# The first of two rank mixes, issued in two halves among the second batch's attention heads

## The chip, the core and the metric

The program runs on one core of a Trainium2 chip. The core has a matrix engine (TensorE, PE in the profile, with its weight loads as PEld), a vector engine (DVE), a scalar engine (ACT), a general engine (POOL) and an engine that here only issues transfers (SP). The four compute engines each take their own list of instructions in order and wait for one another by semaphores. PE writes only to PSUM, a small memory of eight banks, from which DVE and ACT fetch results. The metric is the device time of one execution in microseconds; the kernel before took 1562.12 us as the median of three runs (1556.07 to 1563.89).

## What is computed

Four batches of 448 tokens and 12 heads of width 64 go through attention with normalised queries and keys, then through two mixers. The first mixer adds a low-rank mix over the tokens (rank 32) and then a two-layer network over the 768 channels; the second has a 256-wide token network and a second channel network.

```python
q_n, k_n = rmsnorm(q, g_q), rmsnorm(k, g_k)
attn = softmax(q_n @ k_n.T / 8)            # 4 batches x 12 heads, 448 x 448
x = attn @ v                               # as (4, 448, 768)
u = x + ((x.T @ U) @ V).T                  # the rank mix, U 448x32, V 32x448
x = u + relu(u @ w_ch1) @ w_ch2            # 768 -> 3072 -> 768
u = x + (relu(x.T @ w_tok1) @ w_tok2).T
x = u + relu(u @ w_ch1b) @ w_ch2b          # 768 -> 1536 -> 768
```

The weights arrive as 64-bit floats, and the kernel turns each piece into a pair of 32-bit numbers, a high and a low part.

## The kernel before, in words

Batches are called first to fourth here, heads are counted from 0 over all batches, so heads 0 to 11 are the first batch's and heads 12 to 23 the second's. `attention` walks the heads one step at a time. In step t it issues the softmax of head t+1 (`softmax`: four tiles of scores `sc`, a maximum `nm` on DVE L334, the exponential `p` on ACT L336, and on POOL the scaling L343) next to the weighing of head t (`weigh`: transposes of `p` into `pt`, copies `ph` and `pl` by ACT and DVE, products `pv`), and every second step it loads and normalises a pair of heads ahead of time. The result goes into `xT`, channels by tokens, six pieces of 128 channels; the pieces 0 to 2 are heads 0 to 5 of a batch, the pieces 3 to 5 are heads 6 to 11.

`rank_mix` works in two halves of three pieces. Per half: four times three transposes of `xT` into PSUM (`pt_x`, L432), each evicted as a high part by ACT (L438) and a low part by DVE (L439); two products each into `ps_h`; a copy of `ps_h` by ACT (L461) and a subtraction by DVE (L462); six products into three tiles `ps_u`; and for each of these an addition into `xT` on DVE (L443), a copy `u` on ACT (L444) and a subtraction on POOL (L445).

In the part of the program that matters here, the heads 0 to 23 run first, alone, with PSUM pools `s` (three banks, for `sc`), `t` (one) and `p` (four, for `pt` and `pv`). The factors U and V (`uv`) are loaded in step 8 and sit in two of the four pairs of weight buffers `wh`/`wl`. After step 23 these pools are closed, others are opened with two banks in `p` and two in `s`, and both rank mixes are issued, the first batch's and then the second's. Then `ffn` begins with the first group of the channel network: two pieces of its first weight (`w1_chunk`), two of its second (`w2_chunk`), products `ps_g` for the first batch and then `ps_x`, while the third batch's heads go on among them. A weight piece is made by `to_f32` and `split`: ACT L125 and L130, DVE L126, L127 and L131, POOL L134, then ACT L144 and POOL L145. Since `uv` holds two of the four weight buffers, the two `w2` pieces go into the buffers that the U factors and the V factors leave, which is after the last `ps_h` and after the last `ps_u` of the second rank mix.

The order of the instructions on each engine is not the order of the code. A scheduler decides it at build time by its own estimate of when each instruction can run. Buffers, PSUM banks among them, are handed out in the order of the code, so a tile that is asked for later waits until the earlier holders of its buffer are done.

Of the kernel before, what the change touches and what calls it, by code (L numbers as in the profile page):

```python
# [10 lines left out]
F32R = mybir.dt.float32r  # L11
# [13 lines left out]
def attention_then_two_mixers(  # L25
# [31 lines left out]
    P = 128  # L57
    B, H, S, D = q.shape
# [7 lines left out]
    HALF = DM // 2  # L66
# [8 lines left out]
    def f(x):  # L75
        return x.bitcast(F32)

    def mm(o, l, r, start, stop):
        nc.tensor.matmul(o, lhsT=l, rhs=r, start=start, stop=stop)  # L79
# [20 lines left out]
    pools = {"late": False, "split_u": nc.gpsimd}  # L100
    AT = dict(qr=2, kr=2, vr=3, qn=1, vs=2, p=8, ph=3, pl=3, sq=1)

    def open_pools(stack, side):
        for nm, bufs, space in side:
            pools[nm] = stack.enter_context(tc.tile_pool(
                name=nm, bufs=bufs, **({"space": PSUM} if space else {}), reuse_waits="tile"))

    def psum(kind, shape, name):
        pool = pools[kind]
        return pool.tile(shape, F32, tag=pool.name, name=name)  # L110
# [317 lines left out]
    def to_tokens(xT, hf):  # L428
        for c in range(NC4):
            pt = psum("p", [CP, HALF], "pt_x")  # L430
            for i in range(3):
                nc.tensor.transpose(  # L432
                    pt[:, i * P:(i + 1) * P],
                    xT[:, 3 * hf + i, c * CP:(c + 1) * CP], ident,
                )
            s = pools["new_xs"]()[:CP, :, :HALF]
            hi, lo = s[:, 0], s[:, 1]
            nc.scalar.activation(hi, pt, AF.Copy)  # L438
            nc.vector.tensor_sub(lo, pt, f(hi))  # L439
            yield hi, lo  # L440
# [6 lines left out]
    def new_u():  # L447
        return [act.tile([P, CC, S], F32R, tag=t, name="u") for t in ("uh", "ul")]

    def rank_mix(xT, uv):  # L450

        u4, vh, vl = uv
        u = new_u()
        for hf in range(2):
            ph = psum("t", [P, HALF], "ps_h")
            for c, xs in enumerate(to_tokens(xT, hf)):
                for i in range(2):
                    mm(ph, u4[:, c].rearrange("p t r -> p (t r)"), xs[i],
                       c == 0 and i == 0, c == NC4 - 1 and i == 1)
            hst = pools["new_xs"]()[:, 0, :HALF]  # L460
            nc.scalar.activation(hst, ph, AF.Copy)  # L461
            nc.vector.tensor_sub(hst[2 * R:], ph[2 * R:], f(hst[2 * R:]))  # L462
            for i in range(3):
                pu = psum("s", [P, S], "ps_u")
                hs = hst[:, i * P:(i + 1) * P]
                mm(pu, hs, vh, True, False)
                mm(pu, hs, vl, False, True)
                split_u(xT, 3 * hf + i, pu, u)
        return u

    def token_mix(xT, w):

# [253 lines left out]
    def new_x():  # L726
        return act.tile([P, CC, S], F32, tag="xT", name="xT")
# [14 lines left out]
    xs = [new_x() for _ in range(2)]  # L742
    us = [None] * 2
# [5 lines left out]
    with ExitStack() as stack:  # L749
        open_pools(stack, (("hs", 1, 0), ("at", 2, 0)))  # L750
        inner = stack.enter_context(ExitStack())
        AT.update(p=12, ph=4, pl=4)
        open_pools(inner, (("pp", 1, 0), ("s", 3, 1), ("t", 1, 1), ("p", 4, 1)))
        pools["v"] = pools["p"]

        def new_xo():
            return pools["at"].tile([P, S], F32, tag="xo", bufs=1, name="xo")
# [8 lines left out]
        for t in att:  # L766
            if t == 8:
                pools["late"] = True
                uv = load_uv(False)
                pools["late"] = False  # L770
            if t == 2 * H - 1:
                break
        pools["late"] = True
# [4 lines left out]
        open_pools(stack, (("pp", 1, 0), ("g", 2 * G + 1, 0), ("p", 2, 1), ("v", 1, 1),  # L778
                           ("s", 2, 1), ("t", 1, 1), ("m", 2, 1)))
        pools["new_xs"] = lambda: pools["g"].tile([P, 2, S], F32R, tag="g", name="xs")  # L780
        for i in range(2):
            us[i] = rank_mix(xs[i], uv)


        def mix(i):
# [31 lines left out]
    new_xs = [x3]  # L817
# [46 lines left out]
```

## Time and profile before

| what | value |
|---|---|
| median of three runs | 1562.12 us |
| the profiled execution | 1557.47 us, its span 1555.7 us |
| PE busy over the span | 1468.6 us (94%) |
| DVE, ACT, POOL busy | 1112.0, 709.4, 813.2 us |
| last product of head 23 begins | 198.48 us |
| first weight products of the second group begin | 258.16 us |

A row in order of time gives the start, the duration, the engine, the line, what is written from what, the shapes and the count; in brackets the idle time ahead of it and what ended it. A row of a group gives the busy time and mean of one instruction over the whole span. A row by stretch gives the busy time of each engine between two times, the clock granted to PE as a share of the full one, the share of the transfer engines, and GB/s.

### The profile page before, as it was taken

What the parts mean: (1) busy time and instruction counts of PE and PEld (TensorE: products, weight loads), DVE (VectorE), ACT (ScalarE), POOL (GpSimd) and SP (SyncE); (2) the same over time, 40 slices, a digit from 0 to 9 for tenths busy, and PEclk for the clock granted to TensorE, in tenths of its full rate; (3) what the DMA queues carried; (4) which work ended last, traced back from release to release, by engine and by line L of the source; (5) the groups of instructions that cost most, each with busy time, mean ns of one, the idle gap of its engine ahead of it and who ended that gap; (6) DMA issues with size and microseconds to landing.
All of it is one profiled execution on the core that took longest, in us unless ns stands there. A gap on an engine that the chain in (4) does not pass through costs nothing.

```text
span 1555.7 us, 21597 instructions
## 1 busy us (share of the span) xinstructions
PE 1468.6 (94%) x7522; PEld 1296.6 (83%) x7522; DVE 1112.0 (71%) x1805; ACT 709.4 (46%) x1413; POOL 813.2 (52%) x839
## 2 busy tenths in 40 slices
PE   4999978999999999999999999899999999999998
PEld 3766667788888899898898998789999999988997
DVE  6888887888887888666958776586766665577653
ACT  4767656566666665444634443332322222342311
POOL 6878977777886665444735552042433523113420
PEclk9999989999999999999999999999999999999999
DMA  6665654656654544542515531411212111101202
GB/s 166 151 155 140 159 167 133 183 156 194 192 171 150 150 138 135 183 149 85 186 45 184 181 132 34 160 51 52 71 52 71 51 48 55 66 21 51 72 21 92
DMA packets 96588, 180.94 MB, mean 116 GB/s; under 512 B 8992, under 2 KB 66304, under 8 KB 96480
## 3 DMA queue, kind: packets, MB, share of 16 engines
q1 hardware_dynamic: 96160, 179.57, 37.6%
q8 instruction: 59, 0.97, 0.3%
q14 instruction: 49, 0.40, 0.1%
q10 hardware_dynamic: 320, 0.00, 0.0%
HBM read 107.19 MB, written 36.57 MB: 92 GB/s over the span
## 4 chain that ended last, share of the span: by engine, by line
PE 64%; DVE 11%; POOL 10%; DMA 6%; issue 4%; ACT 4%; SPq 1%; ACTq 0%; DVEq 0%; POOLq 0%
PE ps_x L79 26%; PE ps_g L79 14%; PE ps_p L79 11%; PE sc L79 3%; PE pv L79 2%; POOL w_bits L134 2%; POOL p L343 2%; PE pt L362 2%; PE ps_u L79 2%; POOL w L145 2%; PE ps_t L79 2%; DVE w_bits L126 1%; POOL sq L256 1%; DMA qr<-in_q_dram 1%; DMA ks<-both 1%
## 5 line engine op out<-in xcount | busy, mean ns | idle before, releaser
L79 PE MATMUL ps_x<-gs,w 128*128 128x448 f32 x2592 | 576.1, 370 | 14.7 <-DVE xT L536 4.9
L79 PEld LDWEIGHTS ps_x<-gs,w 128*128 128x128 f32 x2592 | 482.8, 189 | 61.0 <-DVE xT L536 8.7
L79 PE MATMUL ps_g<-u,w 128*128 128x448 f32 x1584 | 343.4, 369 | 1.1 <-POOL u L445 0.9
L79 PEld LDWEIGHTS ps_g<-u,w 128*128 128x128 f32 x1584 | 295.6, 189 | 26.3 <-POOL u L445 1.2
L145 POOL TENSOR_TENSOR w<-w 128x768 fp32r<-128x768 f32 x44 | 86.3, 1970 | 222.0 <-ACT w L144 127.5
L134 POOL TENSOR_TENSOR w_bits<-w_bits,w_round 128x768 uint32<-128x768 uint32 (+3 forms) x80 | 143.7, 1796 | 102.1 <-DVE w_bits L131 41.3
L145 POOL TENSOR_TENSOR w<-w_bits,w 128x768 fp32r<-128x768 f32 (+3 forms) x82 | 147.7, 1808 | 77.9 <-ACT w L144 74.3
L666 DVE TENSOR_TENSOR xT<-ps_x,xT 128x448 f32<-128x448 f32 x216 | 128.1, 617 | 64.1 <-PE ps_x L79 62.9
L536 DVE TENSOR_TENSOR xT<-ps_x,xT 128x448 f32<-128x448 f32 x216 | 132.1, 616 | 37.5 <-PE ps_x L79 34.8
L336 ACT ACTIVATE p<-sc,nm 112x448 f32<-112x448 f32 x192 | 121.3, 634 | 57.5 <-DVE nm L334 52.9
L343 POOL TENSOR_SCALAR p<-p,sm 112x448 f32<-112x448 f32 x192 | 133.9, 710 | 20.3 <-DVE sm L340 18.3
L79 PE MATMUL sc<-ks,qs 128*112 128x448 f32 x384 | 121.0, 408 | 22.2 <-DMA ks<-both 11.0
L145 POOL TENSOR_TENSOR w_a<-w_a 128x384 fp32r<-128x384 f32 (+1 forms) x28 | 42.2, 1507 | 180.9 <-DVE w_t L223 139.4
L334 DVE TENSOR_REDUCE nm<-sc 112x1 f32<-112x448 f32 x192 | 116.3, 613 | 23.9 <-PE sc L79 23.0
L362 PEld LDWEIGHTS pt<-ident,p 112*112 112x112 f32 x768 | 90.5, 136 | 38.1 <-issue 11.6
L362 PE MATMUL pt<-ident,p 112*112 112x112 f32 x768 | 112.9, 263 | 4.9 <-POOL p L343 4.2
L637 DVE TENSOR_TENSOR pu<-ps_p,pu 128x448 f32<-128x448 f32 x98 | 59.2, 619 | 70.4 <-PE ps_p L79 70.3
L126 DVE TENSOR_SCALAR w_bits<-w_bits 128x768 f32<-128x768 f32 (+3 forms) x80 | 77.2, 966 | 43.5 <-ACT w_bits L125 43.0
L373 ACT ACTIVATE ph<-pt 112x448 fp32r<-112x448 f32 (+1 forms) x168 | 88.6, 545 | 31.8 <-PE pt L362 30.7
L130 ACT ACTIVATE w_round<-w_raw 128x768 uint32<-128x768 uint32 (+3 forms) x80 | 69.8, 872 | 72.1 <-POOL w_bits L134 68.9
L377 DVE TENSOR_TENSOR pl<-pt,ph 112x448 fp32r<-112x448 f32 x144 | 87.2, 613 | 10.4 <-ACT ph L373 9.8
L125 ACT ACTIVATE w_bits<-w_raw 128x768 f32<-128x768 f32 (+3 forms) x80 | 69.9, 876 | 51.9 <-POOL w L145 37.8
(111 smaller groups left out, 2297.8 us busy)
## 6 DMA issues: line engine op xcount, KB each, us to landing
w_raw<-in_moe_w_ch_dram SPq DMA_DIRECT2D x72, 768.0 KB, 4.5
ks<-both SPq DMA_DIRECT2D x92, 224.0 KB, 3.8
c_a<-w_bits SPq DMA_DIRECT2D x48, 384.0 KB, 3.1
qs<-both SPq DMA_DIRECT2D x96, 112.0 KB, 2.8
w<-c_a SPq DMA_DIRECT2D x28, 384.0 KB, 3.6
c_b<-w_bits SPq DMA_DIRECT2D x24, 384.0 KB, 3.1
w_a<-c_a SPq DMA_DIRECT2D x20, 384.0 KB, 2.9
w<-c_b SPq DMA_DIRECT2D x16, 384.0 KB, 3.5
```

What stands on the lines that cost most here:

```text
L79: nc.tensor.matmul(o, lhsT=l, rhs=r, start=start, stop=stop)
L126: nc.vector.tensor_scalar_max(f(w), f(w), TINY)
L134: nc.gpsimd.tensor_tensor(w, w, r, op=ALU.add)
L145: nc.gpsimd.tensor_sub(lo, w, f(hi))
L334: nc.vector.tensor_reduce(nm, sc, axis=AX.X, op=ALU.max, negate=True)
L336: nc.scalar.activation(p, sc, AF.Exp, bias=nm, accum_out=sm[:, c % 2:c % 2 + 1])
L343: nc.gpsimd.tensor_scalar(x, x, sm[:, i:i + 1], 1.0, op0=ALU.mult, op1=ALU.mult)
L362: nc.tensor.transpose(pt[:, c * CP:(c + 1) * CP], pr[c][:, kc * CP:(kc + 1) * CP], ident[:CP, :CP],)
L373: nc.scalar.activation(ph, pt, AF.Copy)
L377: nc.vector.tensor_sub(pl, pt, f(ph))
L536: nc.vector.tensor_add(xT[:, dc], px, xT[:, dc])
L666: nc.vector.tensor_add(xT[:, dc], px, xT[:, dc])
```

## The change

`rank_mix` becomes a generator `rank_steps` that stops after each half, and takes the name of the PSUM pool for `ps_h`. For the first batch the output buffers are asked for in step 12, and a half is issued after step 13 and after step 16, with `ps_h` in pool `p` instead of `t` and with three small buffers of its own (`xl`) for the evicted pieces. After step 23 only the second batch's rank mix is issued. Nothing of the arithmetic changes.

```diff
--- before.py
+++ after.py
@@ -448,11 +448,16 @@
         return [act.tile([P, CC, S], F32R, tag=t, name="u") for t in ("uh", "ul")]
 
     def rank_mix(xT, uv):
+        u = new_u()
+        for _ in rank_steps(xT, uv, u, "t"):
+            pass
+        return u
+
+    def rank_steps(xT, uv, u, bank):
 
         u4, vh, vl = uv
-        u = new_u()
         for hf in range(2):
-            ph = psum("t", [P, HALF], "ps_h")
+            ph = psum(bank, [P, HALF], "ps_h")
             for c, xs in enumerate(to_tokens(xT, hf)):
                 for i in range(2):
                     mm(ph, u4[:, c].rearrange("p t r -> p (t r)"), xs[i],
@@ -466,7 +471,7 @@
                 mm(pu, hs, vh, True, False)
                 mm(pu, hs, vl, False, True)
                 split_u(xT, 3 * hf + i, pu, u)
-        return u
+            yield
 
     def token_mix(xT, w):
 
@@ -752,6 +757,8 @@
         AT.update(p=12, ph=4, pl=4)
         open_pools(inner, (("pp", 1, 0), ("s", 3, 1), ("t", 1, 1), ("p", 4, 1)))
         pools["v"] = pools["p"]
+        open_pools(inner, (("xl", 3, 0),))
+        pools["new_xs"] = lambda: pools["xl"].tile([P, 2, HALF], F32R, tag="xl", name="xs")
 
         def new_xo():
             return pools["at"].tile([P, S], F32, tag="xo", bufs=1, name="xo")
@@ -768,6 +775,11 @@
                 pools["late"] = True
                 uv = load_uv(False)
                 pools["late"] = False
+            if t == H:
+                us[0] = new_u()
+                mixing = rank_steps(xs[0], uv, us[0], "p")
+            if t in (H + 1, H + 4):
+                next(mixing)
             if t == 2 * H - 1:
                 break
         pools["late"] = True
@@ -778,8 +790,7 @@
         open_pools(stack, (("pp", 1, 0), ("g", 2 * G + 1, 0), ("p", 2, 1), ("v", 1, 1),
                            ("s", 2, 1), ("t", 1, 1), ("m", 2, 1)))
         pools["new_xs"] = lambda: pools["g"].tile([P, 2, S], F32R, tag="g", name="xs")
-        for i in range(2):
-            us[i] = rank_mix(xs[i], uv)
+        us[1] = rank_mix(xs[1], uv)
 
 
         def mix(i):
```

On PE, among the heads of the second batch, this stands before. It is the second half of the weighing of head 14 and the beginning of that of head 15 (from the row with six transposes `pt` on), with six and again six score products of heads 16 and 17, three tiles each time, between them:

```order
L362 MATMUL pt<-ident,p 112x112 x4
L293 MATMUL tt<-ident,qn 128x112 x4
L79 MATMUL pv<-ph,vr 128x448
L362 MATMUL pt<-ident,p 112x112 x4
L79 MATMUL sc<-ks,qs 112x448 x6
L79 MATMUL pv<-ph,vr 128x448
L362 MATMUL pt<-ident,p 112x112 x6
L293 MATMUL tt<-ident,kn 128x112 x4
L362 MATMUL pt<-ident,p 112x112 x2
L79 MATMUL pv<-ph,vr 128x448
L79 MATMUL sc<-ks,qs 112x448 x6
```

In the changed kernel, at the same heads, the six `ps_u` of the first half stand behind the weighing of head 14, and the scores come behind them:

```order
L362 MATMUL pt<-ident,p 112x112 x4
L79 MATMUL pv<-ph,vr 128x448
L79 MATMUL ps_u<-w,xs 128x448 x6
L293 MATMUL tt<-ident,qn 128x112 x4
L79 MATMUL pv<-ph,vr 128x448
L79 MATMUL sc<-ks,qs 112x448 x20
L362 MATMUL pt<-ident,p 112x112 x2
L79 MATMUL sc<-ks,qs 112x448 x2
L362 MATMUL pt<-ident,p 112x112 x2
L79 MATMUL sc<-ks,qs 112x448 x2
L362 MATMUL pt<-ident,p 112x112 x4
```

The scores of head 15, which stood among the weighing of head 12 before, and those of heads 16 and 17 now follow in one run of 24 products (20, 2 and 2), and the transposes of head 15 begin behind the twentieth. The second half, three steps on, has the same form: six `ps_u`, then 18 score products in a row.

On POOL, behind the last head of the second batch, this stands before (L134 and L145 make weight pieces, L445 is the rank mix, `qn` and `sq` belong to the third batch's heads):

```order
L445 TENSOR_TENSOR u<-xT,u 128x448 x3
L134 TENSOR_TENSOR w_bits<-w_bits,w_round 128x768
L145 TENSOR_TENSOR w<-w_bits,w 128x768
L134 TENSOR_TENSOR w_bits<-w_bits,w_round 128x768
L445 TENSOR_TENSOR u<-xT,u 128x448 x3
L134 TENSOR_TENSOR w_bits<-w_bits,w_round 128x768
L445 TENSOR_TENSOR u<-xT,u 128x448 x3
L145 TENSOR_TENSOR w<-w_bits,w 128x768
L275 TENSOR_TENSOR qn<-qr,rs 112x2x4x64
L445 TENSOR_TENSOR u<-xT,u 128x448
L145 TENSOR_TENSOR w<-w_bits,w 128x768
```

And this in the changed kernel, beginning behind the first weight piece's two instructions:

```order
L445 TENSOR_TENSOR u<-xT,u 128x448 x2
L134 TENSOR_TENSOR w_bits<-w_bits,w_round 128x768
L445 TENSOR_TENSOR u<-xT,u 128x448
L145 TENSOR_TENSOR w<-w_bits,w 128x768
L134 TENSOR_TENSOR w_bits<-w_bits,w_round 128x768
L445 TENSOR_TENSOR u<-xT,u 128x448
L275 TENSOR_TENSOR qn<-qr,rs 112x2x4x64
L145 TENSOR_TENSOR w<-w_bits,w 128x768
L134 TENSOR_TENSOR w_bits<-w_bits,w_round 128x768
L445 TENSOR_TENSOR u<-xT,u 128x448 x2
L256 TENSOR_TENSOR sq<-qr 112x512
L145 TENSOR_TENSOR w<-w_bits,w 128x768
```

Up to the L145 of the fourth weight piece there stood ten L445, two more behind it; now there are six, and none behind.

## Rows read from the trace of the kernel before

**Rows 1.** Busy time by engine in three stretches; the header names the columns.

```profile
core 0: us, PE busy (x) PEld busy (x) DVE busy (x) ACT busy (x) POOL busy (x), PEclk, DMA share, GB/s
123.00:198.50 75.50, 70.06 (x398) 50.81 (x396) 62.13 (x127) 53.83 (x143) 66.17 (x125) 0.98 0.68 170
198.50:258.00 59.50, 44.41 (x191) 36.56 (x192) 49.41 (x70) 33.66 (x64) 42.05 (x36) 0.83 0.45 139
```

**Rows 2.** PE in order of time: start us, us, engine, line, tile, count, [idle before].

```profile
139.91 0.41 PE L79 MATMUL pv<-ph,vs 112*128 112x448 f32 x1
164.94 0.99 PE L79 MATMUL pv<-ph,vr 112*128 112x448 f32 x2
...
198.48 0.47 PE L79 MATMUL pv<-pl,vs 112*128 112x448 f32 x1 [0.19 <-DVE pl L377]
248.42 0.72 PE L79 MATMUL sc<-ks,qs 128*112 128x448 f32 x2 [4.26 <-ACT p L336]
258.16 3.08 PE L79 MATMUL ps_g<-u,w 128*128 128x448 f32 x14
```

**Rows 3.** Costliest groups, whole span: busy us, mean ns, idle before and its releasers.

```profile
L443 DVE TENSOR_TENSOR xT<-ps_u,xT 128x448 f32<-128x448 f32 x48 | 29.0, 617 | 13.0 <-PE ps_u L79 13.0
L444 ACT ACTIVATE u<-xT 128x448 fp32r<-128x448 f32 x48 | 27.5, 575 | 50.5 <-DVE xT L443 50.4
L445 POOL TENSOR_TENSOR u<-xT,u 128x448 fp32r<-128x448 f32 x24 | 30.6, 1291 | 22.3 <-ACT u L444 22.2
L439 DVE TENSOR_TENSOR xs<-pt_x,xs 112x384 fp32r<-112x384 f32 x64 | 33.8, 550 | 13.7 <-ACT xs L438 13.5
L438 ACT ACTIVATE xs<-pt_x 112x384 fp32r<-112x384 f32 x64 | 29.4, 488 | 25.4 <-PE pt_x L432 22.3 <-PE ps_u L79 1.5 <-issue 1.3
L343 POOL TENSOR_SCALAR p<-p,sm 112x448 f32<-112x448 f32 x192 | 133.9, 710 | 20.3 <-DVE sm L340 18.3 <-PE pt L362 0.5 <-PE tt L293 0.2
```

**Rows 4.** PE in order of time, at the full clock, first batch's second half.

```profile
222.93 1.07 PE L79 MATMUL ps_u<-w,xs 128*128 128x448 f32 x4 [2.36 <-DVE xs L462]
223.84 0.69 PE L79 MATMUL ps_h<-xs,w 112*128 112x384 f32 x3
224.37 0.49 PE L432 MATMUL pt_x<-ident,xT 128*112 128x128 f32 x3
224.62 0.45 PE L79 MATMUL ps_g<-u,w 128*128 128x448 f32 x1
```

**Rows 5.** ACT in order of time, two softmax tiles one behind the other.

```profile
137.60 0.63 ACT L336 ACTIVATE p<-sc,nm 112x448 f32<-112x448 f32 x1
138.21 0.63 ACT L336 ACTIVATE p<-sc,nm 112x448 f32<-112x448 f32 x1
```

**Rows 6.** Busy time by engine and granted clock in three shorter stretches.

```profile
139.00:165.00 26.00, 23.07 (x122) 16.62 (x120) 21.73 (x46) 19.31 (x54) 21.51 (x43) 0.93 0.60 151
142.00:147.00 5.00, 4.82 (x20) 3.79 (x21) 5.00 (x12) 3.27 (x9) 3.45 (x7) 0.66 0.85 194
200.00:205.00 5.00, 1.30 (x3) 0.91 (x4) 4.66 (x7) 2.32 (x5) 4.40 (x3) 0.61 0.11 23
```

**Rows 7.** POOL in order of time while the first weights are made.

```profile
203.58 1.81 POOL L134 TENSOR_TENSOR w_bits<-w_bits,w_round 128x768 uint32<-128x768 uint32 x1
213.24 1.14 POOL L445 TENSOR_TENSOR u<-xT,u 128x448 fp32r<-128x448 f32 x1 [3.08 <-ACT u L444]
...
234.62 3.35 POOL L445 TENSOR_TENSOR u<-xT,u 128x448 fp32r<-128x448 f32 x3 [1.49 <-ACT u L444]
242.74 1.83 POOL L145 TENSOR_TENSOR w<-w_bits,w 128x768 fp32r<-128x768 f32 x1
```

**Rows 8.** Busy time by engine while POOL makes the first weights.

```profile
203.58:244.57 40.99, 33.70 (x149) 27.85 (x149) 32.13 (x46) 24.92 (x46) 30.47 (x27) 0.82 0.43 146
```

**Rows 9.** DVE in order of time: the same instruction of L126 at two times.

```profile
212.47 0.55 DVE L126 TENSOR_SCALAR w_bits<-w_bits 128x768 f32<-128x768 f32 x1
242.25 4.82 DVE L126 TENSOR_SCALAR w_bits<-w_bits 128x768 f32<-128x768 f32 x1
```

## The prediction, made before the changed kernel was run

> **What bounds the kernel now.** I read the page's slices first: PE is busy almost throughout except near the start and in the sixth slice, around 200 us, so the change works at the seam that costs most. Then the busy times by stretch. While the second batch's heads run after the first batch is complete, every engine is nearly full [rows 1]: of 75.5 us PE is busy 70.1, POOL 66.2, DVE 62.1 and ACT 53.8. There is no free engine in that stretch; 5.4 us of PE, 9.3 of POOL and 13.4 of DVE are all that can be filled. Behind it, from the last product of head 23 at 198.48 to the second group of weight products at 258.16, some 59 us pass [rows 2], and PE is busy for 44.4 of 59.5 us with a granted clock of 0.83 [rows 1]. Two things run there in one another's way: the two rank mixes, one behind the other, and the making of the first four weight pieces. The chain of waits through this stretch changes between both: copies on ACT, subtractions on DVE, weight conversion on POOL. The point that opens it is the fourth weight piece: its POOL instruction begins at 242.74 and takes 1.83 [rows 7], so it is ready at 244.6, which is 45.6 us after the last product of head 23 (198.48 plus 0.47). Only behind it can `ps_x` run freely, and 13.6 us later the second group begins [rows 2].
>
> **What is moved, and its price.** One rank mix is 24 transposes `pt_x`, 16 `ps_h` and 12 `ps_u` on PE. From starts that follow each other closely [rows 4], four `ps_u` take 0.91, three `ps_h` 0.53 and three transposes 0.25 us, so 12 x 0.23 + 16 x 0.18 + 8 x 0.25 = 7.5 us. On DVE there are 8 low parts of 0.55, two subtractions of `ps_h` (priced as L439) and 6 additions of 0.62: 9.2 us. On ACT 10 copies of 0.49 and 6 of 0.58: 8.3 us. On POOL 6 subtractions of 1.29: 7.7 us [rows 3]. No transfer is moved; `uv` was already loaded in step 8. All this leaves the seam and enters the stretch of the second batch's heads.
>
> **The stretch of heads: a cost.** The order rows show what the code does not say: a half's three `ps_u` are asked for from pool `s` before the scores of the head two steps ahead, so these scores wait until all three are added into `xT`. Before, softmax ran two to three heads ahead of the weighing; at each of the two halves this lead is used up. Behind the first half PE has ten score tiles to do before it may transpose head 15. Tiles follow at ACT's pace, 0.61 us from start to start [rows 5]: 6.1 us, and 1.4 for two scalings of L343 at 0.70 behind the tile that ends it [rows 3], 7.5 us. PE's own part of that is ten tiles of two products of 0.23 [rows 4], 4.6 us, so it stands still for 2.9 us, twice: 5.8. Behind the weighing instruction that waits stand all later products on PE, and ACT's and DVE's copies of `pt`. Against it, the heads that follow have their probabilities ready and can be weighed one behind the other; I let that fill the 2.9 us for which PE was idle from 139 to 165 [rows 6]. For the clock I add 1.0: a stretch of small waits held it at 0.66 over 5 us, which is 1.7 us of work lost [rows 6], and I take about a third of that for each half. Sum: 7.5 + 5.8 - 2.9 + 1.0 = 11.4 us longer. Bounds: 2.1 if only PE's work counts and fills all idle time (70.1 + 7.5 against 75.5), and 26.5 if nothing is given back (7.5 for the score run, 3.75 for half of the PE work and 2.0 for a clock as between 200 and 205, at 0.61 for 5 us [rows 6], twice). A loss of nothing, or a gain, is excluded by PE alone.
>
> **The seam: a gain.** The first weight piece reaches POOL at 203.58, 4.6 us after the last product, and POOL is done with the fourth 41.0 us later. Of these it is busy for 30.5 and waits for 10.5 [rows 8]; four waits for the rank mixes, of 3.08 to 1.49 us, make up 7.8 of them [rows 7]. Behind the change the same list holds eight conversions of 1.8, six subtractions of 1.29 and two normalisations of the third batch of about 1.0 each, 24.3 us. With half of the waits, since there is half of the mixing, it lasts 24.3 + 5.2 = 29.5, so the fourth piece is ready 11.5 us earlier. The weight buffers do not hold it up for longer: the V factors are free after the last `ps_u`, which stands earlier in the same order. `ps_g` of the first batch no longer waits for its `u`. Up to the second group ten score tiles are done instead of seven, 3 x 0.46 = 1.4 us of work ahead. Gain: 12.9 us. Bounds: 41.0 - 24.3 + 1.4 = 18.1 with no wait left, and 4 x 1.29 + 1.4 = 6.6 if only POOL's own work is saved. I take the middle since half of the waits is the nearest reading.
>
> At one place a page bears on the seam. DVE's L126 took 0.55 us at 212.47 and 4.82 at 242.25, while POOL worked without a pause [rows 7, 9], and PE then waited 4.26 us for a score tile behind it [rows 2]. The Trainium skill (SBUF — State Buffer, Who interferes with whom) says that DVE in its faster two-port modes and POOL hold a common port for a whole instruction, and that the second one waits. The trace agrees at this row; by it fewer POOL instructions there mean fewer such stalls, and a rival below takes that.
>
> **The sum.** 11.4 - 12.9 = -1.5 us. The profiled execution took 1557.47, its span 1555.7, so it would take 1556.0; the median of the three runs, 1562.12, lies 4.65 above the profiled one, within their spread. On the median I forecast 1561, no change: work goes from one full stretch to another.
>
> **Rivals.**
> Faster: the heads absorb the work. For it speaks the idle time of DVE and ACT there and that pair preparation (`sq`, `qn`) can run in the score gaps; against it that PE and POOL have only 5.4 and 9.3 us free. With 2.1 + 1.0 and the seam at 17 the sum is -14 us: 1548.
> Slower: the lead of the softmax is lost for good at each half, because behind it POOL and ACT, and not PE, limit the heads, so that scores done together save nothing later. Then 26.5 - 12.9 = +13.6: 1576. It decides when the weighing of head 18, at 164.94 before [rows 2], comes more than 18 us later. For it: no engine has much idle time. Against it: the weighing of heads 15 to 17 took from 139.91 to 164.94 [rows 2], 25 us with the scores of later heads among it, and has room to close up.
> The seam is held by conversion, not by the mixing: DVE, busy 32.1 of 41.0 us [rows 8], keeps its long weight instructions and POOL waits as before. The gain is then 6.6 and the sum +4.8: 1567.
> The long stall at 242.25 goes as well: 4.3 us more gained, the sum -5.8: 1556. The page on the common port is what speaks for it; against it, eight conversions stay on POOL beside the same DVE instructions.
> A clock that falls is part of the slower case. The Trainium skill (TensorE: Matmul & The Clock Gate, HAM oscillation — how this bites in real kernels) warns that bursts of matmuls with waits between them let the clock fall back each time; here 0.66 and 0.61 [rows 6] agree with that, and it speaks against putting two waits into a stretch that now has 0.98 [rows 1].
> That the change does not do what it says is excluded by the order rows.
>
> **Chances.** The forecast 0.34 (own range 1553 to 1569), the heads absorb it 0.24, the lead lost 0.22, conversion holds the seam 0.14, the stall goes 0.06. Half a per cent is 7.8 us, about what a measurement of this kernel can tell from no change: 1554.3 to 1569.9. Faster: 0.23 from the absorbing case, 0.05 from the forecast, 0.02 from the stall, 0.30. Slower: 0.20 from the lost lead, 0.05 from the conversion, 0.02 from the forecast, 0.27. Same: 0.43. The range goes from 1547, just past the absorbing case, to 1576, the middle of the lost lead; about a tenth lies outside on either side.
>
> **What would show it.** In the profile after: runs of some ten score tiles on PE at 0.6 us each behind `ps_u`, at about 141 and 167 us, with PE idle about 3 us before the next `pt`; the last product of head 23 at about 210 instead of 198.5; the fourth weight piece about 34 us behind it instead of 45.6; the second weight group about 46 to 47 us behind it instead of 59. The forecast is wrong if the heads end before 204 or after 218, or if the seam lasts as long as before.

## The result: 10 us slower, and the profile after

The changed kernel took 1568.0 us as the median of six runs (1566.15 to 1570.7), the kernel before beside it 1559.8 (six runs): a ratio of 1.0061, 95% interval 1.0041 to 1.008, so 6 to 12 us slower. No change was forecast, -1.5 us.

First the stretches of [rows 1], now cut where the work is cut: at the last product of head 11, the last of head 23, the 49th `ps_g` (the second weight group), and the 577th `ps_g` (where all 48 heads are done in both kernels). The kernel before, in these bounds:

```profile
core 0: us, PE busy (x) PEld busy (x) DVE busy (x) ACT busy (x) POOL busy (x), PEclk, DMA share, GB/s
120.95:198.95 78.00, 72.55 (x406) 52.37 (x406) 62.99 (x129) 56.07 (x150) 68.22 (x128) 0.98 0.66 166
198.95:260.67 61.72, 46.64 (x204) 38.86 (x205) 50.96 (x73) 35.85 (x70) 44.43 (x39) 0.83 0.46 146
260.67:614.34 353.67, 344.32 (x1896) 307.43 (x1895) 290.35 (x495) 224.14 (x463) 249.80 (x273) 1.00 0.53 161
614.34:1555.60 941.26, 911.01 (x4539) 828.20 (x4537) 615.77 (x922) 317.24 (x526) 359.59 (x227) 0.99 0.26 89
```

The changed kernel:

```profile
117.78:217.20 99.42, 87.17 (x458) 61.02 (x458) 74.87 (x147) 64.14 (x167) 77.57 (x140) 0.95 0.54 133
217.20:269.34 52.14, 39.60 (x167) 32.87 (x167) 43.05 (x62) 30.97 (x57) 37.49 (x34) 0.84 0.55 178
269.34:623.62 354.28, 343.06 (x1881) 305.25 (x1880) 287.37 (x489) 222.15 (x457) 250.28 (x267) 1.00 0.54 163
623.62:1567.20 943.58, 914.38 (x4539) 832.09 (x4537) 613.39 (x921) 317.54 (x526) 357.77 (x227) 0.99 0.26 87
```

The heads of the second batch take 21.4 us longer, the seam 9.6 less, the long stretch behind it 0.6 more, the rest 2.3 more; the part ahead of head 12 is 3.2 shorter. That part and the rest are the kernels' own scatter: over all kernels of this study the rest lasted 938.8 to 945.9 us, and six kernels whose order is that of before up to the seam (e11 to e14, e17, e18) end head 11 between 116.8 and 119.6, not at 120.95.

These rows also give an account that the prediction did not draw up. PE is the engine that is full, so time is PE's work plus what PE loses: the time in which it is not busy, and (1 - PEclk) of the time in which it is, since at the lower of its two levels half of the speed is missing. I call the sum its loss. Among the heads it is 5.45 + 0.02 x 72.55 = 6.9 us before and 12.25 + 0.05 x 87.17 = 16.6 after, 9.7 more. In the seam it is 15.08 + 0.17 x 46.64 = 23.0 before and 12.54 + 0.16 x 39.60 = 18.9 after, only 4.1 less. The other 5.5 us by which the seam is shorter are work of PE: the 52 instructions of the mix have left it for the heads, and some 15 others have come in from the stretch behind (204 to 167 in the seam, 1896 to 1881 behind it).

PE among the heads at the first half, and at the ends of the two stretches, answering to [rows 2]:

```profile
136.25 1.49 PE L79 MATMUL ps_u<-w,xs 128*128 128x448 f32 x6 [0.42 <-DVE xs L467]
...
138.38 1.75 PE L79 MATMUL sc<-ks,qs 128*112 128x448 f32 x6
141.26 1.90 PE L79 MATMUL sc<-ks,qs 128*112 128x448 f32 x6 [1.13 <-ACT p L336]
143.44 1.89 PE L79 MATMUL sc<-ks,qs 128*112 128x448 f32 x6 [0.29 <-ACT p L336]
...
148.74 0.40 PE L362 MATMUL pt<-ident,p 112*112 112x112 f32 x2 [0.76 <-POOL p L343]
...
151.85 0.98 PE L293 MATMUL tt<-ident,kn 112*128 112x112 f32 x4 [2.08 <-DVE both L301]
...
182.50 0.92 PE L79 MATMUL pv<-ph,vr 112*128 112x448 f32 x2
...
216.72 0.48 PE L79 MATMUL pv<-pl,vs 112*128 112x448 f32 x1
...
266.88 3.46 PE L79 MATMUL ps_g<-u,w 128*128 128x448 f32 x16
```

The score run stands where the order put it, at ACT's pace, and head 18 is weighed from 182.50 instead of 164.94. POOL's waits for the mix and for DVE, its fourth weight piece, and two DVE instructions in the seam, the second one the longest there, answering to [rows 7, 9]:

```profile
228.64 1.14 POOL L445 TENSOR_TENSOR u<-xT,u 128x448 fp32r<-128x448 f32 x1 [1.59 <-ACT u L444]
230.69 1.16 POOL L445 TENSOR_TENSOR u<-xT,u 128x448 fp32r<-128x448 f32 x1 [0.92 <-ACT u L444]
234.00 1.81 POOL L134 TENSOR_TENSOR w_bits<-w_bits,w_round 128x768 uint32<-128x768 uint32 x1 [2.15 <-DVE w_bits L131]
...
243.24 1.16 POOL L445 TENSOR_TENSOR u<-xT,u 128x448 fp32r<-128x448 f32 x1 [1.17 <-ACT u L444]
244.35 1.36 POOL L275 TENSOR_TENSOR qn<-qr,rs 112x512 f32<-112x512 f32 x1
...
254.93 1.83 POOL L145 TENSOR_TENSOR w<-w_bits,w 128x768 fp32r<-128x768 f32 x1
```

```profile
243.47 1.34 DVE L127 TENSOR_SCALAR w_bits<-w_bits 128x768 uint32<-128x768 uint32 x1
244.85 3.48 DVE L131 SCALAR_TENSOR_TENSOR w_bits<-w_raw,w_bits 128x768 uint32<-128x768 uint32 x1
```

The piece is ready 39.6 us behind the last product (254.93 + 1.83 - 217.20), not 34. POOL's list from the first weight piece to the fourth, answering to [rows 8]:

```profile
222.45:256.76 34.31, 23.74 (x96) 19.09 (x95) 28.22 (x35) 19.50 (x35) 25.08 (x17) 0.85 0.52 175
```

It lasts 34.3 us instead of 41.0, and POOL waits for 9.2 of them instead of 10.5.

### The profile page after: what moved, and what is told of

Its sections match the earlier page's. It is cut to its first block, busy times and chain, and to the rows that moved or that the text cites. A ratio compares the mean times of both kernels' runs of the same rounds, so it can differ in the third digit from the quotient of the medians.

```text
span 1567.3 us, 21599 instructions
## 1 busy us (share of the span) xinstructions
PE 1476.0 (94%) x7522; PEld 1299.2 (83%) x7522; DVE 1111.0 (71%) x1805; ACT 710.8 (45%) x1413; POOL 813.8 (52%) x839
## 4 chain that ended last, share of the span: by engine, by line
PE 60%; DVE 9%; POOL 5%; ACT 3%; DMA 3%; issue 2%; SPq 0%; DVEq 0%; POOLq 0%; ACTq 0%
PE ps_x L79 26%; PE ps_g L79 15%; PE ps_p L79 11%; POOL w_bits L134 2%; PE ps_t L79 2%; PE ps_u L79 1%; POOL w L145 1%; PE sc L79 1%; PE pv L79 1%; DVE w_bits L126 1%; PE pt L362 1%; DVE w_bits L131 1%; DVE w_bits L127 1%; ACT w L144 1%; ACT w_bits L125 1%
## 5 line engine op out<-in xcount | busy, mean ns | idle before, releaser
L145 POOL TENSOR_TENSOR w<-w 128x768 fp32r<-128x768 f32 x44 | 85.5, 1950 | 221.2 <-ACT w L144 195.7
L134 POOL TENSOR_TENSOR w_bits<-w_bits,w_round 128x768 uint32<-128x768 uint32 (+3 forms) x80 | 142.7, 1784 | 97.0 <-DVE w_bits L131 42.0
L145 POOL TENSOR_TENSOR w<-w_bits,w 128x768 fp32r<-128x768 f32 (+3 forms) x82 | 147.8, 1809 | 78.1 <-ACT w L144 72.8
L79 PE MATMUL sc<-ks,qs 128*112 128x448 f32 x384 | 120.1, 411 | 23.6 <-DMA ks<-both 11.5
L145 POOL TENSOR_TENSOR w_a<-w_a 128x384 fp32r<-128x384 f32 (+1 forms) x28 | 42.5, 1519 | 183.3 <-DVE w_t L223 138.6
L362 PEld LDWEIGHTS pt<-ident,p 112*112 112x112 f32 x768 | 89.9, 136 | 33.7 <-issue 12.6
L126 DVE TENSOR_SCALAR w_bits<-w_bits 128x768 f32<-128x768 f32 (+3 forms) x80 | 71.8, 898 | 49.9 <-ACT w_bits L125 49.8
L79 PEld LDWEIGHTS sc<-ks,qs 128*112 128x112 f32 x384 | 61.3, 186 | 44.3 <-ACT p L336 26.7
L131 DVE SCALAR_TENSOR_TENSOR w_bits<-w_raw,w_bits 128x768 uint32<-128x768 uint32 (+3 forms) x80 | 96.6, 1208 | 1.3
```

Of the source, the lines that this page charges most:

```text
L126: nc.vector.tensor_scalar_max(f(w), f(w), TINY)
L131: nc.vector.scalar_tensor_tensor(w, high, 0xC0000000, w, op0=ALU.bitwise_and, op1=ALU.bitwise_or)
L134: nc.gpsimd.tensor_tensor(w, w, r, op=ALU.add)
L145: nc.gpsimd.tensor_sub(lo, w, f(hi))
L362: nc.tensor.transpose(pt[:, c * CP:(c + 1) * CP], pr[c][:, kc * CP:(kc + 1) * CP], ident[:CP, :CP],)
```

## The experiments

Ratios are to the kernel before, run beside each; 0.0010 is 1.6 us. The theory that came out of the comparison, A: the three `ps_u` of a half take the banks of pool `s`, the scores queue behind them, the softmax loses its lead. Its rival B: the stretch is full, and 7.5 us of PE and as much on the others lengthen it whatever the bank.

**Other banks (e1, e2).**

```
-                pu = psum("s", [P, S], "ps_u")
+                pu = psum("s" if bank == "t" else "p", [P, S], "ps_u")      # e1; e2: "t" for "p"
```

> The first batch's three tiles ps_u of each half come from PSUM pool p instead of s; nothing else differs from the changed kernel. The scores need then not wait for these three tiles to be added into xT. Theory A (the lead of the softmax is lost because the scores queue behind ps_u for the banks of pool s): the run of 20 score products is gone, the stretch from the end of head 11 to the last product of head 23 falls from 97 to about 86 us, the seam stays near 50, and the time is about 1557, 0.993 of the changed kernel's. Rival B (the stretch is simply full: 7.5 us of PE, 9.2 of DVE, 8.3 of ACT and 7.7 of POOL more lengthen it whatever bank they use): the stretch stays at 95 to 98 us and the time at 1568.

> The same tiles ps_u come from pool t instead, which has one bank (and is also used by the transposes of the pair preparation), so they follow one another through it while s and p are left to the heads. Theory A: as with pool p, the stretch of heads falls to 86 to 90 us and the time to 1557 to 1561. Rival B: the stretch stays at 95 to 98 us and the time at 1568. If pool p helps and pool t does not, the holding of any PSUM bank at that place decides, not pool s.

Measured: e1 1.0065 (1.0043 to 1.0087), e2 1.0075 (1.0047 to 1.0103): no better than the change. What PE waits for among the heads (total us, times, longest): for ACT in front of scores before, then the two largest waits in the changed kernel and in e1:

```profile
PE sc L79 <- ACT p L336: 0.9, 2, 0.7
```

```profile
PE sc L79 <- ACT p L336: 6.7, 7, 2.0
PE tt L293 <- DVE both L301: 2.1, 1, 2.1
```

```profile
PE pv L79 <- ACT ph L373: 4.4, 5, 1.6
PE sc L79 <- ACT p L336: 1.7, 4, 0.6
```

The wait that A names did go, from 6.7 to 1.7 us, and another took its place, products waiting for ACT's copies. The heads fell from 99.4 to 93.3 us, the seam rose from 52.1 to 57.8 (granted clock 0.76), and the time stayed. A is right about the wait and wrong about the time: taking this wait away does not bring the time back.

**Half of it, and none of it (e3, e4).** e3 issues the first half alone among the heads and the second in the seam. e4 leaves the mix out but for its last step:

```
+        if bank == "p":
+            for hf in range(2):
+                for cc in range(3 * hf, 3 * hf + 3):
+                    nc.scalar.activation(u[0][:, cc], xT[:, cc], AF.Copy)
+                    nc.gpsimd.tensor_sub(u[1][:, cc], xT[:, cc], f(u[0][:, cc]))
+                yield
+            return
```

> Only the first half of the first batch's rank mix is issued among the heads; the second half is issued behind head 23, as in the kernel before. Theory A: one loss of the lead instead of two, so the stretch of heads is about 86 us (half of the 22 us added), the seam about 54.5, and the time about 1563. Rival B gives the same to within 2 us, since it has half of the work. What it tells: whether the cost comes per half (then 86) or with the first half alone (then 90 or more), or with the second (then under 82).

> The first batch's rank mix is left out but for its last step: at the two places among the heads u is only copied (ACT) and its low part subtracted (POOL) from the attention's result; transposes, products and additions of this mix are not done, so the output lacks it. This isolates the seam and what the bare copies cost among the heads. Theory A and rival B alike: the seam near 50 us as in the changed kernel, the stretch of heads 76 to 80 us, the time 1547 to 1553. If the seam is then much shorter than 50, the moved mix still holds it; if the heads still take over 85, neither the banks nor PE's work but the copies on ACT and POOL are what lengthens them.

Measured: e3 1.0072 (1.0054 to 1.009), as much as both halves, which neither theory had. e4 1.0008 (0.9991 to 1.0024): no faster than before, though 52 instructions of PE are gone and both theories had 1547 to 1553. Heads and seam in e4:

```profile
119.75:205.46 85.71, 76.35 (x415) 56.01 (x413) 66.33 (x135) 58.63 (x156) 69.50 (x131) 0.94 0.65 166
205.46:256.01 50.55, 38.56 (x161) 31.12 (x161) 39.71 (x60) 28.97 (x56) 39.02 (x36) 0.83 0.57 186
```

PE's loss among the heads is 9.36 + 0.06 x 76.35 = 13.9 us, twice that of before, and they take 7.7 us longer than before, with no mixing there at all. Even the copies are hardly there: the scheduler put five of the six between 48.9 and 103.2 us, among the first batch's heads, and from about 50 us on the order differs from that of before. And without any first mix the seam still loses 11.99 + 0.17 x 38.56 = 18.5: most of its 23 us was never the first mix's.

**Taken out of the seam, done twice, in small pieces, at the end (e5 to e8).** Theory C: PE's work costs where it stands, and the seam owes little idle time to the mix. Theory D: the seam hides the mix.

```
-        for i in range(2):                                  # e5, on the kernel before
-            us[i] = rank_mix(xs[i], uv)
+        us[0] = new_u()
+        for cc in range(CC):
+            nc.scalar.activation(us[0][0][:, cc], xs[0][:, cc], AF.Copy)
+            nc.gpsimd.tensor_sub(us[0][1][:, cc], xs[0][:, cc], f(us[0][0][:, cc]))
+        us[1] = rank_mix(xs[1], uv)
-        us[1] = rank_mix(xs[1], uv)                         # e6, on the changed kernel
+        for i in range(2):
+            us[i] = rank_mix(xs[i], uv)
-            if t in (H + 1, H + 4):                         # e8
+            if t in (2 * H - 2, 2 * H - 1):
```

e7 adds a `yield` behind each of the first three sets of transposes and ahead of each `ps_u`, and takes one or two steps of it per head.

> The kernel before, with the first batch's rank mix left out behind head 23 but for its last step (u copied by ACT, its low part subtracted by POOL); its transposes, products and additions are not done, so the output lacks them. Nothing is issued among the heads. With the time before this gives what the first mix costs in the seam. Theory C (PE's account: the mix is 7.5 us of PE work wherever it stands, and the seam owes only 3 to 5 us of its idle time to it): 10 to 12 us less than before, about 1547. Rival D (in the seam the mix lies beside the conversion of the weights and is hidden): 0 to 3 us less, about 1556.

> The changed kernel, with the first batch's rank mix issued a second time behind head 23, where it stood before, so the mix is done twice and the output holds it twice. With the time before this gives what the mix costs among the heads. Theory C: 20 to 22 us more than before, about 1579, and the changed kernel's loss of 10 is this cost less the seam's saving. Rival D: what is repeated in the seam is hidden there, so about 10 to 12 us more than before, 1568 to 1570.

> The first batch's rank mix is issued in fourteen small pieces over the steps 13 to 21 instead of two halves (each set of three transposes with its two or four ps_h products, and each ps_u, by itself), with ps_u in pool p. If the lumps are what costs (a half brings eight evictions and three additions at once, which stand in front of the heads' own on ACT and DVE), PE's idle time among the heads falls from 12 us to 6 or 7 and the time is 1560 to 1562. If the engines' added work costs wherever it stands, the heads stay 92 to 98 us long and the time at 1567 to 1569.

> The two halves are issued after the steps 22 and 23 instead of 13 and 16, so at the end of the stretch of heads, where no scores follow that could lose their lead, and still in the pools of the heads. Theory C: PE's work stays in the tail and the seam; the idle time of some 5 us right behind the last product of head 23 is filled by the transposes and ps_h of this mix, so 3 to 5 us less than before, 1553 to 1555. Rival: the seam is held by the conversion of the weights, whatever PE does in it, and the time is that of before, 1557 to 1559. Over 1563 would say that any mix issued ahead of the last product costs.

Measured: e5 1.0000 (0.9984 to 1.0016), e6 1.0154 (1.0135 to 1.0174), e7 1.0045 (1.0026 to 1.0064, its runs from 1558 to 1572), e8 1.0079 (1.0062 to 1.0095). e6 speaks for C (20 to 22 us), 24 us where D had 10 to 12; against the changed kernel it puts a mix in the seam at 14.5 us. e5 decides nothing between C and D: its trace has on all four engines the same instructions in the same order as e4, so to the engines the two are one program. What the pair tells is how well things repeat: 1.0008 and 1.0000 in time, and a loss of 13.9 and 14.6 us among the heads and of 18.5 and 20.2 in the seam, and 11.8 and 15.2 us of idle time behind it, so that 2 us in the first two and 3 to 4 behind the seam are no more than scatter. e7 says that the lumps are a part at most; PE's idle time among its heads is 12.4 us, where the lumps as the cause asked for 6 or 7. e8 is over the 1563 that it named for "any mix issued ahead of the last product costs". It keeps the order of before up to 187 us and yet loses: the loss among its heads is 13.3, and in the stretch behind the seam PE is idle for 14.8 us instead of 9.4.

**Order alone (e9, e10), and the mix out of the seam with the order kept (e11).** Every kernel so far but e8 had the heads in another order than before, even where little or nothing was added to them. Theory E: that order is what costs. The controls change one number and no work:

```
-            if t == 8:
+            if t == 9:                                      # e9; e10: 6; e16: 9, on the changed kernel
-        for i in range(2):                                  # e11
-            us[i] = rank_mix(xs[i], uv)
+        us[0] = us[1] = rank_mix(xs[1], uv)
```

> A control: the kernel before, with the factors U and V loaded in step 9 instead of 8 and nothing else. The same work; but the scheduler lays out the heads from about head 7 on in another order, as it does for every kernel of this study except the late one. Theory E (the order of the kernel before is an unusually tight one, and any other order of the heads costs about as much as the change did): 1565 to 1569, with PE's idle and half-clock time among the heads 13 to 17 us instead of 7. Theory C (the mix among the heads is what costs): 1556 to 1562.

> The same control with the factors loaded in step 6, which gives a third order of the heads. Theory E: 1565 to 1569 again. Theory C: 1556 to 1562. If one control is slow and the other is not, orders of the same work differ by some 8 us among themselves, and a single difference of 8 us can't be put down to the mix alone.

> The kernel before, with the first batch's rank mix left out altogether: its first network reads the second batch's u, so the output lacks this mix. Unlike the earlier removal in the seam no copy is left that could slip among the heads, and up to the seam every engine's order is that of the kernel before. What the mix costs in the seam, by itself: theory C (7.5 us of PE work and 3 to 5 us of idle time) 1546 to 1549; theory D (hidden beside the conversion) 1556 to 1559.

Measured: e9 1.0039 (1.0023 to 1.0055), e10 1.0116 (1.0089 to 1.0142), e11 0.9968 (0.9947 to 0.9988). The two controls do exactly the work of before and are 6 and 18 us slower, one less and one more than E had. Heads and seam of e10:

```profile
115.90:201.10 85.20, 72.88 (x408) 52.95 (x407) 65.06 (x131) 57.96 (x155) 67.29 (x125) 0.97 0.64 156
201.10:267.00 65.90, 48.82 (x200) 40.42 (x200) 47.71 (x67) 32.09 (x63) 42.72 (x41) 0.76 0.38 123
```

The loss among its heads is 12.3 + 2.2 = 14.5 us instead of 6.9, and that is less than half of the 18 us: the seam loses 28.8 instead of 23.0, and behind it PE is idle for 16.8 us instead of 9.4. In e9 the heads lose 10.0. So the order of before is a tight one, and the two others that were tried are dearer, by 0.6 and 1.9 times the whole effect. e11 has before's order up to the seam (heads 78.2 us long) and gives the seam's part by itself: 5.0 us (1.9 to 8.3) for the whole first mix, between what C (1546 to 1549) and D (1556 to 1559) had, and less than the 7.5 us of PE work that it leaves out. Seam, and the stretch behind it:

```profile
195.30:262.26 66.96, 48.69 (x204) 39.86 (x203) 53.58 (x77) 36.32 (x75) 48.97 (x48) 0.80 0.54 162
262.26:606.64 344.38, 336.55 (x1846) 299.85 (x1844) 275.71 (x476) 216.41 (x441) 241.12 (x258) 1.00 0.53 160
```

With a whole mix less this seam is 5 us longer than that of before: other work has moved into it (204 instructions again, although 52 of the mix are gone), and the stretch behind it is 9 us shorter. The length of the seam is therefore no measure of a gain.

**What holds the seam (e12 to e15, e17, e18), and the changed kernel in another order (e16).**

```
+        pools["n"] = pools.get("n", 0) + 1                  # e13, in to_f32, behind the first copy
+        if 3 <= pools["n"] <= 6:
+            return f(w)
-                us[i] = rank_mix(xs[i], uv)                 # e14; e15: around us[1] of the changed kernel
+                pools["split_u"] = nc.vector
+                us[i] = rank_mix(xs[i], uv)
+                pools["split_u"] = nc.gpsimd
```

e12 takes `ps_h` of every second half from bank `v`; e17 is e14 with e12; e18 is e14 for the second batch's mix alone.

> The kernel before, with ps_h of every second half in the PSUM bank v, which is free until the third batch's heads are weighed, so that a half of a rank mix need not wait until the half before it has left the one bank t. Nothing moves out of the seam. If the idle time of PE in the seam (15 us, and 8.6 lost at half clock) comes from the mixes' chain through that bank, 3 to 6 us less than before, 1553 to 1556; if it comes from the weights' conversion, no change, 1557 to 1561.

> The kernel before, with the conversion of the first four weight pieces behind head 23 cut down: DVE's three instructions and POOL's addition for each are left out (ACT's copies, the split and the transfers stay), so these weights and the output are wrong in value. PE's work is the same and its order nearly so. If the conversion holds the seam, PE's idle and half-clock time there falls from 24 to 14 us or less and the time by 6 to 10 us, to 1548 to 1552. If the chains of the two rank mixes hold it, the seam keeps 21 to 24 us of it and the time is 1555 to 1559.

> The kernel before, with the subtraction that ends both rank mixes behind head 23 moved from POOL (twelve of 1.29 us) to DVE (0.6 us each). Nothing moves in place. If the seam is held by POOL's list, or by DVE instructions that wait beside POOL, 3 to 6 us less than before, 1552 to 1555; if DVE is the fuller one there, 7 us more on it make the seam longer: 1560 to 1565.

> The same edit on the changed kernel, for the six subtractions of the second batch's mix. If POOL holds the seam, 2 to 3 us less than the changed kernel, 1565; otherwise 1568 to 1571.

> The changed kernel with the factors U and V loaded in step 9 instead of 8, as in the first control: the same work in another order of the heads from about head 9 on. Theory C (the mix among the heads costs by itself, whatever the order): 1566 to 1571, as the changed kernel. Theory E (orders of the same work differ by as much as the effect): the time lies more than 4 us from the changed kernel's, in either direction.

> The kernel before with two edits: the rank mixes' subtraction behind head 23 on DVE instead of POOL, and ps_h of every second half in bank v. If the chain through the one bank t shows once POOL is relieved, 2 to 4 us less than with the subtraction alone, 1551 to 1553; if not, as with the subtraction alone, 1554 to 1556.

> The kernel before, with the subtraction moved to DVE for the second batch's mix only, six instead of twelve. If POOL's list while the first pieces are converted is what counts, the first batch's six matter and half or less of the gain is left, 1556; if only the stretch just ahead of the second group counts, all of it, 1554.

Measured: e12 1.0005 (0.9986 to 1.0025), e13 0.9948 (0.9931 to 0.9966), e14 0.9983 (0.9969 to 0.9998), e15 1.0055 (1.0033 to 1.0077), e16 1.0105 (1.0075 to 1.0135), e17 1.0033 (1.0011 to 1.0056), e18 1.0024 (1.0005 to 1.0042). The chain through bank `t` does not hold the seam (e12, between 2 us less and 4 more). The conversion holds a part of it; heads, seam and the stretch behind it in e13:

```profile
119.60:200.00 80.40, 73.59 (x407) 53.79 (x406) 63.05 (x129) 56.77 (x150) 68.30 (x128) 0.96 0.64 162
200.00:253.70 53.70, 44.17 (x205) 36.82 (x205) 37.01 (x61) 32.35 (x66) 35.55 (x35) 0.87 0.52 168
253.70:605.60 351.90, 344.24 (x1896) 307.50 (x1896) 289.71 (x496) 223.97 (x462) 249.87 (x273) 1.00 0.54 162
```

PE's loss in the seam falls from 23.0 to 9.5 + 5.7 = 15.3 us, the seam is 8.0 shorter with the same work in it, and 8.1 us (5.3 to 10.7) of it arrive at the end. Here the gain in the seam is kept. In e17 it is not; its seam and the stretch behind:

```profile
195.51:254.14 58.63, 46.06 (x204) 37.73 (x204) 50.10 (x83) 35.93 (x68) 30.80 (x27) 0.83 0.48 158
254.14:616.45 362.31, 347.76 (x1897) 307.17 (x1896) 293.97 (x497) 225.40 (x464) 252.06 (x273) 1.00 0.53 160
```

PE's loss in the seam falls to 12.6 + 7.8 = 20.4 us, but behind it PE is idle for 14.6 us instead of 9.4, and the whole takes 5 us more, not less. e12, e14, e17 and e18 all have PE's order of before to 207 us or later and lie from 2.7 us below to 5 us above it, so some of e11's 5.0 and e13's 8.1 us may be order, too. e16 is 16 us above the kernel before where the changed one is 10 above: orders of the changed kernel differ by some 7 us, more than the 4 that E asked for.

Of the versions that leave nothing out, e14 alone is faster than the kernel before, by 2.7 us (0.3 to 4.8). DVE's conversions in the seam, first before and then in e14:

```profile
L126 DVE TENSOR_SCALAR w_bits<-w_bits 128x768 f32<-128x768 f32 x6 | 9.1, 1514 | 1.2 <-ACT w_bits L125 1.2
L131 DVE SCALAR_TENSOR_TENSOR w_bits<-w_raw,w_bits 128x768 uint32<-128x768 uint32 x6 | 8.8, 1475 | 0.1
L127 DVE TENSOR_SCALAR w_bits<-w_bits 128x768 uint32<-128x768 uint32 x6 | 5.3, 887 | 0.1
```

```profile
L445 DVE TENSOR_TENSOR u<-xT,u 128x448 fp32r<-128x448 f32 x12 | 10.1, 843 | 0.6 <-ACT u L444 0.6
L131 DVE SCALAR_TENSOR_TENSOR w_bits<-w_raw,w_bits 128x768 uint32<-128x768 uint32 x6 | 6.4, 1067 | 0.0
L126 DVE TENSOR_SCALAR w_bits<-w_bits 128x768 f32<-128x768 f32 x6 | 6.2, 1041 | 1.0 <-ACT w_bits L125 1.0
L127 DVE TENSOR_SCALAR w_bits<-w_bits 128x768 uint32<-128x768 uint32 x6 | 3.3, 550 | 0.0
```

Twelve subtractions that cost POOL 12 x 1.29 = 15.5 us [rows 3] cost DVE 10.1, and the same eighteen conversions take 15.9 instead of 23.2 us on it. The fourth weight piece is hardly earlier for it; POOL's list up to it in e14, answering to [rows 8]:

```profile
200.17:240.76 40.59, 33.68 (x149) 27.57 (x149) 33.75 (x56) 25.20 (x46) 18.43 (x16) 0.82 0.43 148
```

POOL is busy for 12.0 us less, and the list lasts 40.6 us instead of 41.0. On the changed kernel (e15) the same edit makes the piece ready 33.9 us behind head 23 and the seam 47.0 us long, but its time cannot be told from the changed kernel's (1.0055 against 1.0061). And two near relatives, e17 and e18, are slower than before by 0.33 and 0.24%, with both expectations missed, so I take e14 as a small gain of this one order and not as a rule.

## Why the prediction was wrong

**The heads' cost, 11.4 us: this is the step that failed.** The stretch became 21.4 us longer, 10.0 more than the sum, while the seam's term was off by 3.3. The wait that the prediction named is there, and of its size: the score runs stand at 138 and 171 us, and PE's waits for ACT in front of scores rose from 0.9 to 6.7 us, by the 5.8 forecast. What failed is the rest of the sum. The 2.9 us that were to be given back were not: head 18 is weighed 17.6 us later (20.7 counted from the end of head 11), head 23 ends 18 later. PE's idle time rose by 6.8 us, where 5.8 - 2.9 = 2.9 stood, and the half-clock part by 2.9, where 1.0 stood; that 1.0 came from a stretch in which PE was busy for 4.82 of 5.00 us [rows 6], so it is the price of a fallen clock and not of small waits. PE's busy time without the half-clock part rose by 11.7, where 7.5 stood. The mix itself was priced rightly: in the trace its instructions make up 7.2 us of the busy time that no other covers. The rest is on the 399 instructions of the heads themselves, the same in both kernels, busy for 71.7 us before and 79.1 after (70.0 and 74.4 without the half-clock part). Products with waits between them, each showing its full 0.4 us instead of 0.23, would explain it; that was not tested. Nor does the time hang on the wait that was named: e1 took it away, and the time stayed.

**The seam's gain, 12.9 us, came out as 9.6.** It took the fourth weight piece as the point that opens the seam and let half of POOL's waits go with half of the mix. Of the 11.5 us by which that piece was to be earlier, 6.0 came (39.6 instead of 45.6). Halving was right for the waits for the mix, 7.8 us before and 3.7 after, but all 10.5 were halved, and the others rose from 2.7 to 5.6, most of them for DVE and ACT in the conversion itself: 9.2 in all, where 5.2 stood. That POOL's own work sets the time of the piece is not borne out either: e14 takes 12.0 us of it away, and the piece comes 0.5 us earlier. Most of the seam's loss was not the first mix's: without it the seam keeps 18.5 us of PE's loss (e4), and without the conversion of four pieces it keeps 15.3 with both mixes in it (e13). And the length of the seam was counted as if all of it were gain; 5.5 of the 9.6 us were PE's own work. What the mix costs there in time depends on the order: 5.0 us by e11, 14.5 by e6 against the changed kernel.

Neither of the prediction's signs of being wrong came: the last product of head 23 begins at 216.72, between 204 and 218, and the seam is shorter. The cost was set too low and the gain too high, so the two misses add up.

**The rivals.** The slower case, the lead lost for good, misses its own mark by a little (17.6 us against 18) and meets it when counted from the end of head 11 (20.7). It gave 1576; its 26.5 us for the heads are nearer to the 21.4 measured than the forecast's 11.4. The case in which conversion holds the seam gave 1567, close to the 1568.0 measured, but by luck: its sum was 4.8 us above the kernel before, where the change is 9.5 above it, and it had 11.4 for the heads. Its mechanism e13 bears out in part. The stall of DVE did not go: 3.48 us at 244.85.

**What was not on the list at all: the order.** But for the score runs, both sums took the heads' other instructions to stay as they were. By the runs, leaving the mix out of the seam is worth 5.0 us (e11); adding the copies of `u`, which then run among the first batch's heads, with the order that follows from it, takes 5 to 6 back (e5 and e4 against e11), and lengthens the second batch's heads by 7.7 of the 21.4 us; doing the mix there adds 8.3 (the change against e4). Since e9 and e10 show 6 and 18 us from order alone, the last two can't be split cleanly into work and order. That stays open, and so do two more things: why half of the mix among the heads costs as much as all of it (e3), and why PE is idle so much longer behind the seam in e8, whose heads keep their order nearly to the end.

## What to carry to other kernels

On an engine that is busy nine tenths of the time, moving work gains only what that engine then loses less: add up its idle and half-clock time by stage before and after, over all stages (e17 gained in one and lost in the next), and do not take a shorter stage for a gain when work has left it. Before putting down an effect of half a per cent to a cause, build a control that does the same work in another order; here one number, the step at which a small weight is loaded, moved the time by 0.4 and 1.2%. To learn what a stage waits for, leave out the suspect alone, and look in the trace whether the order stayed: the conversion gave back 8 us, the mix 5, and 14.5 in another order.

## What the runs showed of the hardware

DVE's 0.55 us instruction can wait beside POOL across several of POOL's instructions. In e11 DVE and POOL start together:

```profile
222.29 3.80 DVE L126 TENSOR_SCALAR w_bits<-w_bits 128x768 f32<-128x768 f32 x1
226.12 0.56 DVE L127 TENSOR_SCALAR w_bits<-w_bits 128x768 uint32<-128x768 uint32 x1
226.72 3.44 DVE L131 SCALAR_TENSOR_TENSOR w_bits<-w_raw,w_bits 128x768 uint32<-128x768 uint32 x1
```

```profile
222.28 3.39 POOL L445 TENSOR_TENSOR u<-xT,u 128x448 fp32r<-128x448 f32 x3
225.76 0.40 POOL L339 TENSOR_SCALAR sm<-sm 112x2 f32<-112x2 f32 x1
226.24 1.34 POOL L256 TENSOR_TENSOR sq<-qr 112x512 f32<-112x512 f32 x1
227.54 1.80 POOL L145 TENSOR_TENSOR w<-w_bits,w 128x768 fp32r<-128x768 f32 x1
```

POOL's three subtractions end at 225.67 and the conversion at 226.09, 0.42 us behind them; POOL's next pair ends at 229.34 and the third DVE instruction at 230.16, 0.82 behind. The maxima of the softmax stand behind these on DVE, and PE waits 5.5 us for ACT in front of one score tile:

```profile
231.50 0.71 PE L79 MATMUL sc<-ks,qs 128*112 128x448 f32 x1 [5.52 <-ACT p L336]
```

The Trainium skill (SBUF — State Buffer, Who interferes with whom) has DVE's second port pair shared with POOL under an exclusive lock, and these rows agree: both long conversions end 0.4 or 0.8 us behind the end of a POOL instruction. It need not wait for the end of POOL's whole run: in the changed kernel L127 at 243.47 ends at 244.81, 0.41 us behind the first of three POOL instructions that follow each other, and the next one on DVE takes 3.48. What decides how many it waits for, no run here shows. Which instruction is hit, and whether one is, changes from kernel to kernel: the longest took 4.8 us before, 3.5 in the changed kernel, 5.5 in e3, and e9 and e12 had none over 2.5 in the seam with the same instructions.

Among the heads the clock alone does not order the times: the granted clock there was 1.00 in e1's profiled execution, which took 1571.6 us, and 0.92 in e2's, which took 1562.8.
